# Order of the last pass, the token search, weight buffers and final stores in an attention and mixture-of-experts kernel

## The chip, the cores and the metric

The kernel runs on one core of one Trainium2 chip. The time is device microseconds of one execution; lower is better. TensorE (PE) does the matmuls, VectorE (DVE), ScalarE (ACT) and GpSimd (POOL) the rest; SyncE (SP) issues most DMAs, ACT one, and POOL the indexed ones.

## What is computed

```python
def _moe_ref(x, w_gate, w_local, w1, w2):          # x: Nystrom attention's output, 8 x 576 x 512
    ...
    for b in range(B):
        prev_e = -1
        for s in range(S):
            fresh_e = int(np.argmax(logits[b, s]))
            if s == 0 or local_gate[b, s] < 0.5:
                e = fresh_e
            else:
                e = prev_e if prev_e >= 0 else fresh_e
            prev_e = e
            ...
            h = np.maximum(x[b, s] @ w1[e], 0.0)
            out[b, s] = p[e] * (h @ w2[e])
```

The attention part has 32 landmarks per head, a softmax of three score matrices and six Newton steps for a pseudo-inverse. Each token is then sent through one of eight experts (512 to 1024 to 512). In most batches nearly all tokens have the same expert.

## The kernel before

Each batch is run with its own most frequent expert, as two passes over its tokens (`PASSES`): tokens 256 to 575 (blocks 2, 3 and the half block 4), then tokens 0 to 255 (blocks 0 and 1). Tokens with another expert are collected over all batches into slots of 128 tokens, one expert each. With these inputs one slot is enough; its **slot pass** follows the last batch, and a loop for more slots stands behind it (`tc.If(n_slots > 1)`), which is not entered.

A pass has eight steps, one per block `f` of the hidden dimension. Step `f` does `mm1` (six matmuls into a PSUM bank `ph` of which there are two; ACT writes the rectified high part `h` at L938, DVE the low part at L943 and, for the half block, L946) and, a step or two later, `after` (six matmuls into two banks `py`: `wh` with high `h`, `wl` with high `h`, `wh` with low `h`). In the slot pass it is three matmuls. All weights and activations are split into a high and a low float32r part. `split_w2` makes `wh` by a cast on ACT (L918) and `wl` by a subtraction on POOL (L920); `w_w1` folds the attention's weights into the first layer and writes `gh` (ACT) and `gl` (DVE, L906). Raw blocks of w2 have four buffers, `wh` and `wl` eight each.

The order on all engines is written by hand: `at_time(t, fn)` puts an event on a clock that has one unit per step of a pass, 16 per batch (`CH`), and `run` emits what is due before the next step's matmuls. A generator's `yield d` puts its rest `d` units later. Each engine executes its instructions in the order emitted.

For the slot, `slot_tokens` (from L1058) finds on DVE which tokens are in it: a first part up to the registers `xregs` (L1061 to L1070), a second that ends with `row` and `rhs` (L1073 to L1088), five small matmuls (L1092), the addresses `gi` (L1095 to L1108), eight gathers on POOL (L1113), and the transposition of what they brought, `xa` (L1119). `slot_weights` reads the registers on SP and loads `xwt` and w1. Before the change these events stood at

```python
    at_time((B - 1) * CH + 5.5, slot_tokens, sts[B])
    at_time((B - 1) * CH + 6, slots_end)
```

that is, in the first pass of the last batch, and the slot's weights were handled in the second pass. At the end `slot_store` scales the slot's result on ACT and DVE, half each (L1136, L1137), and POOL scatters it to its rows (L1138). Results of whole blocks are scaled on ACT (L1000) and stored by SP (L1002); the half block 4 goes over ACT (L1008, L1009) and POOL (L1011).

Of the kernel before, what the change touches and what calls it, by code (L numbers as in the profile page):

```python
# [23 lines left out]
P = 128  # L24
# [38 lines left out]
def nystrom_attn_then_sticky_moe(ctx, tc, qT, kT, v, wg, w12, out):  # L63
# [821 lines left out]

    def w_w1(st, q, f0=0, nf=4, banks=((pg, "pg"), (ph, "ph"))):

# [11 lines left out]
        if f0 == 0:  # L899
            st["g", q] = [fw.tile([P, 2, 512], F32R, name=f"g{p}", bufs=3) for p in "hl"]  # L900
        gh, gl = st["g", q]
# [11 lines left out]

    def split_w2(w2, f, by=nc.scalar.copy):

        raw = w2[f]
        wh, wl = w2[f] = [fw.tile([P, 512], F32R, name=f"w{p}", bufs=8) for p in "hl"]
        by(out=wh, in_=raw)  # L918
        yield 0.25
        nc.gpsimd.tensor_tensor(out=wl, in0=raw, in1=wh.bitcast(F32), op=ALU.subtract)  # L920

# [69 lines left out]
    def catch_up():  # L991
        run(math.inf)
        while behind:
            behind.pop(0)()

    def store(b, st, k, yp):
        t0 = b * S + k * P
        if k < 4:
            ys = fk.tile([P, DM], F32, name="ys", bufs=2)
            nc.scalar.mul(out=ys, in_=yp, mul=st["pw"][:, k:k + 1])  # L1000
            yield 0.5
            nc.sync.dma_start(out=out[t0:t0 + P, :], in_=ys)  # L1002
        else:
# [54 lines left out]
    def slot_tokens(st):  # L1058
# [26 lines left out]
        for i in range(3, 6):  # L1085
            nc.vector.tensor_copy(out=rhs[:, :, i], in_=p)
            if i < 5:
                nc.vector.tensor_tensor(out=p, in0=p, in1=rhs[:, :, i], op=ALU.subtract)  # L1088
        yield 1.25
        pi = one.tile([P, 6])  # L1090
# [20 lines left out]
        for g in range(2):  # L1111
            for c in range(4):
                nc.gpsimd.indirect_dma_start(out=xa[:, g, c, :], out_offset=None, in_=ad,  # L1113
                                             in_offset=bass.IndirectOffsetOnAxis(ap=gi[:, g, c:c + 1], axis=0),
                                             bounds_check=B * P * 2 * NJ - 1, oob_is_err=False)
        yield 6.5
        px = one.tile([P, 2, P])
# [5 lines left out]

    def slot_weights(st):
        e = expert_of(xregs[0:1, 0:1])
        b = nc.values_load(xregs[0:1, 1:2], engines=[ET.SP], min_val=0, max_val=B - 1,
                           skip_runtime_bounds_check_because="a batch")
        st["wt"] = xp.tile([P, 2, P], F32, name="xwt")
        nc.sync.dma_start(out=st["wt"], in_=wtd[bass.ds(b, 1)].rearrange("a p (g x) -> p (a g) x", g=2))
        for hf in range(2):  # L1130
            st["w1", hf] = load_w1(e, hf)
        return e
# [101 lines left out]
    for b in range(1, B):  # L1234
        attention(b)
    for b in range(1, B + 1):
        t0 = (b - 1) * CH
        for hf in range(2):
            at_time(t0 + (G0, G1)[hf] + ((b == 1) * 1, 1.5 * (b in (B - 2, B - 1)))[hf], lambda b=b, hf=hf: w_w1(sts[b], hf))
        for f in range(NC2):  # L1240
            at_time(t0 + W2 + f + (b == 1), get_w2, b, f)
            at_time(t0 + C2 + 1.75 * (b == 1) + 0.9 * f, cast_w2, b, f)
    for f in range(NC2):
# [21 lines left out]
    def slots_end():  # L1265
        sts[B]["e"] = slot_weights(sts[B])

# [3 lines left out]
    at_time((B - 2) * CH + 11.75, tables, B - 1, 1, 0.5)  # L1271
    at_time((B - 1) * CH + 5.5, slot_tokens, sts[B])
    at_time((B - 1) * CH + 6, slots_end)

    with tc.manual_schedule():
        startup(sts[0], sts[1])
        for b in range(B):
            st = sts[b]
            gen = expert(st, w2s[b], PASSES, lambda k, yp, b=b, st=st: store(b, st, k, yp), b == 0)
            for i in range(CH):  # L1280
                if i % NC2 != 3:
                    clock[0] = b * CH + i
                    run(clock[0])
                next(gen)
        st = sts[B]
        gen = expert(st, w2s[B], ((0, P, (0,)),), lambda k, yp: slot_store(st, k, yp))
        for f in range(NC2):
            if f != 3:
                clock[0] = B * CH + f
                run(clock[0])  # L1290
            next(gen)
        catch_up()
# [34 lines left out]
```

## Time and profile before

| | |
|---|---|
| median of 3 runs | 465.86 us (465.59 to 466.44) |
| the profiled execution | 466.5 us in all, of which the span of its instructions 464.7 us |
| TensorE busy | 446.7 us, 96% of the span |
| VectorE, ScalarE, GpSimd busy | 290.0, 208.8 and 194.1 us |
| granted TensorE clock, mean | 0.996 of full speed |
| DMA | 82.58 MB, 178 GB/s over the span |

All times in the rows below count from the start of the span. Busy time of TensorE is modelled from pipelined matmuls, so that a short hole does not show as idle. The first pass of the last batch runs from 400.6 to about 422, its second pass to 447, the slot pass to 457.3.

### The profile page before, as it was taken

The page shows a single profiled execution, that of the slowest core. Times are in us where ns is not written, and L with a number is a line of the kernel's source. Part 1 is how long each engine was busy: PE and PEld are TensorE (multiplying, and loading weights), DVE is VectorE, ACT ScalarE, POOL GpSimd, SP SyncE. Part 2 cuts the span into 40 slices and gives each one's busy share as a digit, 9 for nine tenths or more (in the row PEclk, how much of TensorE's full clock was granted, in tenths as well). Part 3 has the DMA queues.
Part 4 walks back from the last instruction along what each step waited for, and adds up shares of the span by engine and source line. Part 5 has one row for each costly group of instructions (what it writes and reads, how often), then busy time and mean ns, then how long its engine had stood idle before and what let it go on. Part 6 is the DMA issues. An engine that isn't in the chain of part 4 may idle for free. (4 is left out here: it accounts for less than half of the span.)

```text
span 464.7 us, 12032 instructions
## 1 busy us (share of the span) xinstructions
PE 446.7 (96%) x4688; PEld 338.4 (73%) x4688; DVE 290.0 (62%) x862; ACT 208.8 (45%) x538; POOL 194.1 (42%) x216
## 2 busy tenths in 40 slices
PE   8888999999999999999999999999999999999993
PEld 2435667777787788777887788778878788788772
DVE  7875888767476765857575775857356756335230
ACT  2526435555363724555254724554255414532450
POOL 5455471246343632256235622364016601534561
PEclk9999999999999999999999999999999999999998
DMA  8669925647345851859054941762073305616430
GB/s 305 215 205 333 336 94 175 237 135 279 142 150 202 282 201 44 288 167 329 10 211 162 310 155 50 281 210 91 2 279 120 131 0 202 217 47 214 139 138 21
DMA packets 38812, 82.58 MB, mean 178 GB/s; under 512 B 3243, under 2 KB 4523, under 8 KB 37984
## 3 DMA queue, kind: packets, MB, share of 16 engines
q1 hardware_dynamic: 37184, 76.58, 47.7%
q0 software_dynamic: 1488, 5.07, 3.1%
q8 instruction: 38, 0.62, 0.6%
q14 instruction: 22, 0.18, 0.1%
q10 hardware_dynamic: 80, 0.13, 0.1%
HBM read 66.34 MB, written 15.47 MB: 176 GB/s over the span
## 5 line engine op out<-in xcount | busy, mean ns | idle before, releaser
L973 PE MATMUL py<-wh,h 128*128 128x512 f32 x528 | 171.7, 407 | 0.0
L920 POOL TENSOR_TENSOR wl<-raw,wh 128x512 fp32r<-128x512 f32 x72 | 92.6, 1293 | 95.2 <-ACT wh L918 91.3
L938 ACT ACTIVATE h<-ph 128x256 fp32r<-128x256 f32 (+2 forms) x136 | 54.4, 401 | 162.1 <-PE ph L931 123.3
L973 PEld LDWEIGHTS py<-wh,h 128*128 128x128 f32 x528 | 89.3, 188 | 27.1 <-issue 15.2
L943 DVE SCALAR_TENSOR_TENSOR h<-ph,h 128x256 fp32r<-128x256 f32 (+1 forms) x136 | 55.5, 409 | 81.9 <-ACT h L938 76.3
L973 PE MATMUL py<-wl,h 128*128 128x512 f32 x264 | 83.2, 393 | 0.0
L931 PE MATMUL ph<-ath,gh 128*128 128x320 f32 (+1 forms) x256 | 76.9, 300 | 1.2 <-ACT gh L903 0.6
L931 PE MATMUL ph<-ath,gl 128*128 128x320 f32 (+1 forms) x256 | 75.6, 295 | 0.0
L931 PE MATMUL ph<-atl,gh 128*128 128x320 f32 (+1 forms) x256 | 75.6, 295 | 0.0
L973 PEld LDWEIGHTS py<-wl,h 128*128 128x128 f32 x264 | 49.4, 188 | 11.8 <-POOL wl L920 0.8
L931 PEld LDWEIGHTS ph<-ath,gh 128*128 128x128 f32 x256 | 48.3, 189 | 9.6 <-ACT h L938 1.1
L931 PEld LDWEIGHTS ph<-atl,gh 128*128 128x128 f32 x256 | 48.2, 188 | 4.5
L931 PEld LDWEIGHTS ph<-ath,gl 128*128 128x128 f32 x256 | 48.2, 188 | 0.2 <-DVE gl L906 0.2
L918 ACT CAST wh<-raw 128x512 fp32r<-128x512 f32 x69 | 42.5, 620 | 1.2 <-DMA raw<-w 1.2
L234 POOL TENSOR_TENSOR t<-q_t 128x288 f32<-128x288 f32 x20 | 14.6, 747 | 38.4 <-DVE before L560 27.6
L1011 POOL TENSOR_TENSOR ys<-ys,yl 64x512 f32<-64x512 f32 x8 | 10.3, 1284 | 43.1 <-ACT yl L1009 43.1
L234 POOL TENSOR_TENSOR t<-k_t 128x288 f32<-128x288 f32 x20 | 14.5, 748 | 28.8 <-DVE sq L236 18.1
L906 DVE TENSOR_TENSOR gl<-pg,gh 128x512 fp32r<-128x512 f32 (+2 forms) x19 | 12.4, 655 | 17.4 <-ACT gh L903 17.4
L1000 ACT ACTIVATE ys<-py,token 128x512 f32<-128x512 f32 x32 | 20.3, 686 | 5.8 <-PE py L973 5.8
L982 PE MATMUL pg<-wh,h 128*128 128x512 f32 x56 | 22.0, 392 | 0.0
L982 PE MATMUL pg<-wl,h 128*128 128x512 f32 x56 | 21.9, 391 | 0.0
L492 POOL TENSOR_TENSOR sa<-sa,rsa 128x1152 f32<-128x1152 f32 x7 | 14.9, 2135 | 14.2 <-PE one L445 11.7
(330 smaller groups left out, 702.8 us busy)
## 6 DMA issues: line engine op xcount, KB each, us to landing
raw<-w SPq DMA_DIRECT2D x73, 256.0 KB, 7.3
raw<-w SPq DMA_DIRECT2D x17, 1024.0 KB
v_t<-v SPq DMA_DIRECT2D x8, 1024.0 KB, 5.8
out<-ys SPq DMA_DIRECT2D x32, 256.0 KB, 3.0
q_t<-qT SPq DMA_DIRECT2D x6, 1152.0 KB, 8.3
k_t<-kT SPq DMA_DIRECT2D x6, 1152.0 KB
ad<-sa POOLq DMA_DIRECT2D x8, 576.0 KB
q_t<-qT SPq DMA_DIRECT2D x3, 576.0 KB
```

Source lines behind the costliest of these rows:

```text
L234: nc.gpsimd.tensor_add(t9[:, i], src[:, a + i, :, 0:9], src[:, a + i, :, 9:18])
L492: nc.gpsimd.tensor_tensor(out=sa, in0=sa, in1=rs.unsqueeze(2).broadcast_to([P, 2 * NJ, M]), op=ALU.mult)
L906: nc.vector.tensor_tensor(out=gl[:, g, x], in0=ps[g], in1=gh[:, g, x].bitcast(F32), op=ALU.subtract)
L918: by(out=wh, in_=raw)
L920: nc.gpsimd.tensor_tensor(out=wl, in0=raw, in1=wh.bitcast(F32), op=ALU.subtract)
L931: mm = nc.tensor.matmul(hp, w[:, g, c], x[:, g, s0:s0 + n], start=(i == 0), stop=(i == 5))
L938: nc.scalar.activation(out=h[:, 0:e], in_=hp[:, 0:e], func=AF.Relu)
L943: nc.vector.scalar_tensor_tensor(out=h[:, 384:384 + m], in0=hp[:, 0:m], scalar=0.0, in1=h[:, 0:m].bitcast(F32), op0=ALU.max, op1=ALU.subtract)
L973: nc.tensor.matmul(yps[k], h[:, part + i * P:part + i * P + P], w, start=(f == 0 and part == 0 and w is wh), stop=(f == NC2 - 1 and part = ...
L982: nc.tensor.matmul(yps[4], hs[ff][1], w, start=(ff == 0 and w is w2[ff][0]), stop=(ff == NC2 - 1 and w is w2[ff][1]))
L1000: nc.scalar.mul(out=ys, in_=yp, mul=st["pw"][:, k:k + 1])
L1011: nc.gpsimd.tensor_tensor(out=ys[0:64], in0=ys[0:64], in1=yl[0:64], op=ALU.add)
```

## The change

The slot pass moves between the two passes of the last batch. `slot_tokens` is due 7.25 units earlier (in the second pass of the batch before), `slot_weights` 6.5 units earlier, with the second half of w1 three units after the first. The slot's `w_w1` take PSUM banks of the pool `psa`; its second `gh` and `gl` and its `wh` and `wl` (seven of eight) have buffers of their own in the pool `xp`. For blocks 4 to 7 of the last batch `wl` is made on DVE in place of POOL. The last two results are blocks 0 and 1 of the last batch: block 0 is scaled on DVE and stored by SP, block 1 is scaled on ACT and stored by ACT's own queue. `catch_up` now alternates between events and deferred matmuls.

```diff
@@ -883,7 +883,7 @@
                 "a f p x -> p (a f) x"))
         return t
 
-    def w_w1(st, q, f0=0, nf=4, banks=((pg, "pg"), (ph, "ph"))):
+    def w_w1(st, q, f0=0, nf=4, banks=((pg, "pg"), (ph, "ph")), home=fw):
 
 
         w1 = st["w1", q]
@@ -897,7 +897,7 @@
                 nc.tensor.matmul(ps[g][32 * c:32 * c + 32, :], st["wt"][r, g, 32 * c:32 * c + 32],
                                  w1[r, f0:f0 + nf, a * P:a * P + P], start=True, stop=True)
         if f0 == 0:
-            st["g", q] = [fw.tile([P, 2, 512], F32R, name=f"g{p}", bufs=3) for p in "hl"]
+            st["g", q] = [home.tile([P, 2, 512], F32R, name=f"g{p}", bufs=3 if home is fw else 1) for p in "hl"]
         gh, gl = st["g", q]
         for g in range(2):
             nc.scalar.copy(out=gh[:, g, x], in_=ps[g])
@@ -911,13 +911,13 @@
         nc.sync.dma_start(out=raw, in_=w12[bass.ds(e, 1), f, :, 512:1024].rearrange("a p x -> p (a x)"))
         return raw
 
-    def split_w2(w2, f, by=nc.scalar.copy):
+    def split_w2(w2, f, by=nc.scalar.copy, rest=nc.gpsimd, home=fw):
 
         raw = w2[f]
-        wh, wl = w2[f] = [fw.tile([P, 512], F32R, name=f"w{p}", bufs=8) for p in "hl"]
+        wh, wl = w2[f] = [home.tile([P, 512], F32R, name=f"w{p}", bufs=8 if home is fw else 7) for p in "hl"]
         by(out=wh, in_=raw)
         yield 0.25
-        nc.gpsimd.tensor_tensor(out=wl, in0=raw, in1=wh.bitcast(F32), op=ALU.subtract)
+        rest.tensor_tensor(out=wl, in0=raw, in1=wh.bitcast(F32), op=ALU.subtract)
 
     def mm1(st, hs, f, s0, n, apart):
 
@@ -989,17 +989,21 @@
                 yield
 
     def catch_up():
-        run(math.inf)
-        while behind:
-            behind.pop(0)()
+        while behind or events:
+            run(math.inf)
+            if behind:
+                behind.pop(0)()
 
     def store(b, st, k, yp):
         t0 = b * S + k * P
         if k < 4:
             ys = fk.tile([P, DM], F32, name="ys", bufs=2)
-            nc.scalar.mul(out=ys, in_=yp, mul=st["pw"][:, k:k + 1])
+            if b == B - 1 and k == 0:
+                nc.vector.tensor_scalar(out=ys, in0=yp, scalar1=st["pw"][:, k:k + 1], scalar2=None, op0=ALU.mult)
+            else:
+                nc.scalar.mul(out=ys, in_=yp, mul=st["pw"][:, k:k + 1])
             yield 0.5
-            nc.sync.dma_start(out=out[t0:t0 + P, :], in_=ys)
+            (nc.scalar if b == B - 1 and k == 1 else nc.sync).dma_start(out=out[t0:t0 + P, :], in_=ys)
         else:
             p = st["pw"][0:64, k:k + 1]
             yield 2
@@ -1086,7 +1090,7 @@
             nc.vector.tensor_copy(out=rhs[:, :, i], in_=p)
             if i < 5:
                 nc.vector.tensor_tensor(out=p, in0=p, in1=rhs[:, :, i], op=ALU.subtract)
-        yield 1.25
+        yield 1.75
         pi = one.tile([P, 6])
         for k in range(NBLK):
             nc.tensor.matmul(pi, row[:, k, :], rhs[:, k, :], start=(k == 0), stop=(k == NBLK - 1))
@@ -1113,7 +1117,7 @@
                 nc.gpsimd.indirect_dma_start(out=xa[:, g, c, :], out_offset=None, in_=ad,
                                              in_offset=bass.IndirectOffsetOnAxis(ap=gi[:, g, c:c + 1], axis=0),
                                              bounds_check=B * P * 2 * NJ - 1, oob_is_err=False)
-        yield 6.5
+        yield 5.25
         px = one.tile([P, 2, P])
         for g in range(2):
             nc.tensor.transpose(out=px[:, g, :], in_=xa[:, g].rearrange("p c l -> p (c l)"), identity=ident)
@@ -1121,13 +1125,13 @@
         nc.scalar.copy(out=st["at"][0], in_=px)
         nc.vector.tensor_tensor(out=st["at"][1], in0=px, in1=st["at"][0].bitcast(F32), op=ALU.subtract)
 
-    def slot_weights(st):
+    def slot_weights(st, parts=(0, 1)):
         e = expert_of(xregs[0:1, 0:1])
         b = nc.values_load(xregs[0:1, 1:2], engines=[ET.SP], min_val=0, max_val=B - 1,
                            skip_runtime_bounds_check_because="a batch")
         st["wt"] = xp.tile([P, 2, P], F32, name="xwt")
         nc.sync.dma_start(out=st["wt"], in_=wtd[bass.ds(b, 1)].rearrange("a p (g x) -> p (a g) x", g=2))
-        for hf in range(2):
+        for hf in parts:
             st["w1", hf] = load_w1(e, hf)
         return e
 
@@ -1233,13 +1237,16 @@
     G0, G1, W2, C2 = 13.75, 16.75, 11, 14
     for b in range(1, B):
         attention(b)
-    for b in range(1, B + 1):
+    for b in range(1, B):
         t0 = (b - 1) * CH
         for hf in range(2):
             at_time(t0 + (G0, G1)[hf] + ((b == 1) * 1, 1.5 * (b in (B - 2, B - 1)))[hf], lambda b=b, hf=hf: w_w1(sts[b], hf))
         for f in range(NC2):
             at_time(t0 + W2 + f + (b == 1), get_w2, b, f)
-            at_time(t0 + C2 + 1.75 * (b == 1) + 0.9 * f, cast_w2, b, f)
+            if b == B - 1 and f > 3:
+                at_time(t0 + C2 + 0.9 * f, lambda f=f: split_w2(w2s[B - 1], f, rest=nc.vector))
+            else:
+                at_time(t0 + C2 + 1.75 * (b == 1) + 0.9 * f, cast_w2, b, f)
     for f in range(NC2):
         if f > 3:
             at_time(f - 3, get_w2, 0, f)
@@ -1263,14 +1270,24 @@
         nc.gpsimd.memset(xs["now"], 0.0)
 
     def slots_end():
-        sts[B]["e"] = slot_weights(sts[B])
+        sts[B]["e"] = slot_weights(sts[B], (0,))
+
+    def slot_w1():
+        sts[B]["w1", 1] = load_w1(sts[B]["e"], 1)
 
     xp = None
     at_time((B - 2) * CH + 0.5, slots_begin)
     at_time((B - 2) * CH + 2.5, tables, 0, B - 1, 0.75)
     at_time((B - 2) * CH + 11.75, tables, B - 1, 1, 0.5)
-    at_time((B - 1) * CH + 5.5, slot_tokens, sts[B])
-    at_time((B - 1) * CH + 6, slots_end)
+    last = (B - 1) * CH
+    at_time(last - 1.75, slot_tokens, sts[B])
+    at_time(last - 0.5, slots_end)
+    at_time(last + 2.5, slot_w1)
+    for hf in range(2):
+        at_time(last + (5.25, 8.5)[hf], lambda hf=hf: w_w1(sts[B], hf, banks=((psa, "one"), (psa, "one")), home=(fw, xp)[hf]))
+    for f in range(NC2):
+        at_time(last + 3 + 0.75 * f, get_w2, B, f)
+        at_time(last + 6.25 + 0.75 * f, lambda f=f: split_w2(w2s[B], f, home=xp))
 
     with tc.manual_schedule():
         startup(sts[0], sts[1])
@@ -1278,17 +1295,17 @@
             st = sts[b]
             gen = expert(st, w2s[b], PASSES, lambda k, yp, b=b, st=st: store(b, st, k, yp), b == 0)
             for i in range(CH):
+                if b == B - 1 and i == NC2:
+                    slot = expert(sts[B], w2s[B], ((0, P, (0,)),), lambda k, yp: slot_store(sts[B], k, yp))
+                    for f in range(NC2):
+                        if f != 3:
+                            clock[0] = last + NC2 + f
+                            run(clock[0])
+                        next(slot)
                 if i % NC2 != 3:
-                    clock[0] = b * CH + i
+                    clock[0] = b * CH + i + NC2 * (b == B - 1 and i >= NC2)
                     run(clock[0])
                 next(gen)
-        st = sts[B]
-        gen = expert(st, w2s[B], ((0, P, (0,)),), lambda k, yp: slot_store(st, k, yp))
-        for f in range(NC2):
-            if f != 3:
-                clock[0] = B * CH + f
-                run(clock[0])
-            next(gen)
         catch_up()
     n_slots = nc.values_load(nslot[0:1, 0:1], min_val=0, max_val=E * B * 5)
     with tc.If(n_slots > 1):
```

Lines from L997 on have numbers higher by 4 or more in the changed kernel: the comparison that makes `row` is L1080 before and L1084 after, the small matmuls L1092 and L1096.

The first place is DVE's list where the second pass of the batch before the last ends: `h` rows are low parts of steps, and the row ahead of the first one shown is the second `gl` subtraction. Before:

```order
L906 TENSOR_TENSOR gl_5826<-ph_5816,gh_5825 128x512
L943 SCALAR_TENSOR_TENSOR h_5845<-ph_5838,h_5845 128x256
L943 SCALAR_TENSOR_TENSOR h_5867<-ph_5860,h_5867 128x256
L943 SCALAR_TENSOR_TENSOR h_5889<-ph_5882,h_5889 128x256
L946 SCALAR_TENSOR_TENSOR h_5889<-ph_5882,h_5889 128x64
L943 SCALAR_TENSOR_TENSOR h_5913<-ph_5906,h_5913 128x256
```

After, from the first of these `h` rows on (six operations of the search, L1065 to L1074, now stand between the `gl` row and it):

```order
L943 SCALAR_TENSOR_TENSOR h_5845<-ph_5838,h_5845 128x256
L1077 TENSOR_SCALAR mask_5862<-xslot_5365,xnow_5367 128x40
L1079 TENSOR_TENSOR m3_5864<-token_126,mask_5862 128x120
L1081 TENSOR_REDUCE mine_5866<-m3_5864 128x15
L1084 TENSOR_TENSOR row_5884<-iota128_84,mine_5866 128x640
L1087 TENSOR_TENSOR rhs_5886<-tab_93,mine_5866 128x5x3
L1090 CAST rhs_5886<-mine_5866 128x5
L1092 TENSOR_TENSOR mine_5866<-mine_5866,rhs_5886 128x5
L1090 CAST rhs_5886<-mine_5866 128x5
L1092 TENSOR_TENSOR mine_5866<-mine_5866,rhs_5886 128x5
L1090 CAST rhs_5886<-mine_5866 128x5
L943 SCALAR_TENSOR_TENSOR h_5882<-ph_5875,h_5882 128x256
```

The low part of the next step (`h_5867` before, `h_5882` after) had nothing between it and the step before; now the second part of the search stands there.

The second place is TensorE's list at the same point, between `after` of a step and the next `mm1`. Before:

```order
L973 MATMUL py_5724<-wh_5500,h_5845 128x512
L973 MATMUL py_5725<-wh_5500,h_5845 128x512
L931 MATMUL ph_5906<-ath_5760,gh_5825 128x320
L931 MATMUL ph_5906<-atl_5761,gh_5825 128x320
L931 MATMUL ph_5906<-ath_5760,gl_5826 128x320
```

After:

```order
L973 MATMUL py_5725<-wl_5501,h_5845 128x512
L973 MATMUL py_5724<-wh_5500,h_5845 128x512
L973 MATMUL py_5725<-wh_5500,h_5845 128x512
L1096 LDWEIGHTS row_5884
L1096 MATMUL one_5939<-rhs_5886,row_5884 128x6
```

Four more such pairs of L1096 follow, and then the same `mm1` as before, now into `ph_5946`. The five small matmuls that read `row` and `rhs` came four steps later before; `ph_5906` and `ph_5946` are the bank that the low part `h_5867` or `h_5882` sets free.

The third place is the end of ACT's list. Before:

```order
L938 ACTIVATE h_6479<-ph_6472 128x128
L938 ACTIVATE h_6492<-ph_6485 128x128
L938 ACTIVATE h_6505<-ph_6498 128x128
L1136 ACTIVATE ys_6517<-py_6442,xpw_6143 128x256
L1293 TENSOR_LOAD nslot_129
```

After:

```order
L938 ACTIVATE h_6480<-ph_6473 128x256
L938 ACTIVATE h_6496<-ph_6489 128x256
L1004 ACTIVATE ys_6519<-py_6427,token_126 128x512
L1006 DMA out<-ys_6519 128x512
L1310 TENSOR_LOAD nslot_129
```

Where half a slot tile was scaled for POOL's scatter, a whole block is scaled and stored by ACT itself; DVE's last instruction is likewise a block of 128x512, and SP's last DMA its store.

## Rows read from the trace of the kernel before

**Rows 1.** Busy time by windows, one window: us, busy time of each engine (instructions), clock, DMA, GB/s.
```profile
410.00:420.00 10.00, 10.00 (x52) 8.68 (x51) 3.98 (x16) 1.86 (x5) 3.48 (x3) 1.00 0.00 0
```

**Rows 2.** Timeline of the end: start us, us, engine line operation out<-in, [idle before].
```profile
456.90 0.39 PE L973 MATMUL py<-wh,h 128*128 128x512 f32 x1
457.33 0.47 ACT L1136 ACTIVATE ys<-py,xpw 128x256 f32<-128x256 f32 x1 [1.84 <-PE py L973]
457.90 0.48 DVE L1137 TENSOR_SCALAR ys<-py,xpw 128x256 f32<-128x256 f32 x1 [2.09 <-ACTq L1294]
458.67 1.03 POOL L1138 DMA_INDIRECT out<-ys,tis  x1 [4.87 <-DVE ys L1137]
```

**Rows 3.** Sequencer at L1294 and L1323: ns min/median/max, first and last start us.
```profile
L1294 POOLq INC_SWDGE_SEM  x1: 531/531/531, 461.9 to 461.9; - x1
...
L1323 POOLq DRAIN  x3: 40/107/1462, 462.4 to 464.5; - x3
L1323 SPq DRAIN  x3: 7/7/13, 463.1 to 464.2; - x3
```

**Rows 4.** Tile ys from 400 us on: scaling of whole blocks, landing of stores.
```profile
L1000 ACT ACTIVATE ys<-py,token x6: 680/684/690, 405.1 to 448.1; 128x512 f32<-128x512 f32 x6
...
DMA to landing us min/median/max: 2.1/2.3/3.0
```

**Rows 5.** Timeline of DVE, the token search in its old place.
```profile
416.81 0.14 DVE L1061 TENSOR_SCALAR xnow<-xnow 128x1 f32<-128x1 f32 x1
...
418.24 0.16 DVE L1070 CAST xregs<-xv 1x2 int32<-1x2 f32 x1
...
419.65 0.81 DVE L1080 TENSOR_TENSOR row<-iota,mine 128x640 bf16<-128x640 bf16 x1
...
421.28 0.18 DVE L1086 CAST rhs<-mine 128x5 bf16<-128x5 f32 x1
```

**Rows 6.** Timeline of DVE around the new place of the search.
```profile
396.82 0.68 DVE L906 TENSOR_TENSOR gl<-ph,gh 128x512 fp32r<-128x512 f32 x1
...
399.83 0.42 DVE L943 SCALAR_TENSOR_TENSOR h<-ph,h 128x256 fp32r<-128x256 f32 x1 [0.60 <-ACT h L938]
```

**Rows 7.** Timeline of TensorE, first matmuls of two steps of the last batch.
```profile
402.86 0.30 PE L931 MATMUL ph<-ath,gh 128*128 128x320 f32 x1
...
407.42 0.38 PE L931 MATMUL ph<-ath,gh 128*128 128x320 f32 x1 [0.25 <-DVE h L946]
```

**Rows 8.** Timeline of POOL, splits of the last batch's w2.
```profile
398.57 3.81 POOL L920 TENSOR_TENSOR wl<-raw,wh 128x512 fp32r<-128x512 f32 x3 [6.32 <-ACT wh L918]
402.70 1.30 POOL L920 TENSOR_TENSOR wl<-raw,wh 128x512 fp32r<-128x512 f32 x1 [0.32 <-ACT wh L918]
```

**Rows 9.** Timeline around 391 us, POOL and DVE.
```profile
390.95 1.29 POOL L1011 TENSOR_TENSOR ys<-ys,yl 64x512 f32<-64x512 f32 x1 [19.39 <-ACT yl L1009]
...
391.06 1.21 DVE L1037 TENSOR_SCALAR xend<-xend 128x8 f32<-128x8 f32 x1
```

**Rows 10.** Two lines of DVE over the whole span: ns min/median/max.
```profile
L564 DVE TENSOR_TENSOR ecol<-ecol,low x8: 166/539/547, 29.7 to 383.0; 128x5 int32<-128x5 int32 x8
...
L943 DVE SCALAR_TENSOR_TENSOR h<-ph,h x136: 282/424/426, 38.7 to 455.5; 128x256 fp32r<-128x256 f32 x128, 128x128 fp32r<-128x128 f32 x8
```

**Rows 11.** Timeline of POOL's gathers, first and last of eight, and of DVE.
```profile
423.39 1.10 POOL L1113 DMA_INDIRECT xa<-ad,gi  x1 [7.87 <-DVE fx L1101]
...
432.65 1.00 POOL L1113 DMA_INDIRECT xa<-ad,gi  x1 [0.30 <-issue]
...
423.46 0.16 DVE L1106 TENSOR_TENSOR tis<-fx 128x1 int32<-128x1 f32 x1
```

**Rows 12.** Timeline of ACT, casts of blocks 5 and 6 of the last batch.
```profile
408.90 1.13 ACT L918 CAST wh<-raw 128x512 fp32r<-128x512 f32 x2
```

**Rows 13.** Busy time by windows, two windows after the last matmul: columns as in rows 1.
```profile
457.30:461.00 3.70, 0.00 (x0) 0.00 (x0) 0.48 (x1) 0.47 (x1) 1.03 (x1) 1.00 0.18 63
461.00:464.70 3.70, 0.00 (x0) 0.00 (x0) 0.00 (x0) 0.00 (x0) 0.00 (x0) 0.51 0.01 2
```

## The prediction

> **What bounds the kernel.** I read the windows first: in the last batch TensorE is busy the whole stretch [rows 1], as in every window up to 457. So the time is TensorE's list of work plus the tail behind its last matmul. The change adds and removes no matmul; it can only shorten the tail or open holes in TensorE's list.
>
> The tail comes from the timeline of the end [rows 2] and the sequencer's rows [rows 3]. TensorE ends at 457.29. ACT scales one half of the slot tile from 457.33, DVE the other half to 458.38, POOL issues the scatter to 459.70, and its landing lets POOL go on at 461.9. Then SP works through its list of semaphores (from 462.4, its first drain at 463.1), POOL drains from 462.4 to 463.9, and 0.8 us of barriers end the span at 464.7. The tail is 464.7 - 457.3 = 7.4 us.
>
> **The change, step by step.**
>
> *Plain stores at the end.* The last result is now two blocks of 128x512. Counted from the same point (457.33): ACT scales its block in 0.69 us [rows 4] to 458.02 and issues the store about 0.05 later. DVE scales the other block beside it: 0.48 us for 256 columns [rows 2], so at most 0.96 by twice that, and it starts one matmul (0.23) earlier, so it ends hardly later than ACT. Stores land 2.1 to 3.0 us after issue [rows 4]; two at once move 512 KB, so I take 2.4, which gives 460.5. Then SP's semaphores (462.4 to 463.1, 0.7 us, plus some 0.3 for those ahead of them) and the barriers (0.8): 462.3. POOL's long drain, 1.46 us, is done before, since POOL no longer waits for a scatter. Gain 464.7 - 462.3 = **-2.4**; with landings of 2.1 and 3.0 it is -2.7 and -1.8.
>
> *The token search moves forward.* In the old place DVE ran it from 416.81 to 421.46 [rows 5], 4.65 us with one step's h pieces inside, and POOL idle. Now it stands on DVE right behind the second gl subtraction, which ends at 397.50 [rows 6]; undisturbed it would end at about 402.0, with one h piece inside. TensorE would not feel it: the h piece behind the search (the row at 399.83) would end at 402.4, and the matmul that needs its PSUM bank comes at 402.86 [rows 7].
>
> But in the new place POOL is splitting w2: three subtractions back to back from 398.57 to 402.38, a fourth from 402.70 to 404.00 [rows 8]. The trace shows what that does. A tensor_scalar of 128x8 on DVE took 1.21 us because it started while POOL's addition of 390.95 to 392.24 ran; it ended 0.03 behind it [rows 9]. L564, two inputs in SBUF, takes 0.17 us alone and 0.54 in most batches, where it meets POOL's additions; L943, which has one input in PSUM, never takes over 0.43 [rows 10]. So an operation of DVE with two SBUF inputs, or a tensor_scalar or cast from SBUF to SBUF, waits for the end of the POOL instruction that runs when it comes, and back-to-back POOL instructions catch each one that waits on the one before.
>
> Worked through: the first six operations take 1.59 us [rows 5]; the sixth, the cast to xregs, starts at 398.9 and is held to 399.87. The h piece that stands here follows to 400.3 (it is needed by the last pair of matmuls ahead of 402.86: free). The mask comes into POOL's second split and ends at 401.15, m3 into the third, to 402.5, the sum takes 0.37 to 402.9. The comparison that makes row (0.81) comes into the fourth and ends at about 404.7. The small rest takes 421.46 - 420.46 = 1.0, to 405.7; no fifth split follows, since splits 4 to 7 leave POOL. Then the h piece, 0.42, to 406.1. TensorE wants to go on at 402.86 with the five small matmuls that read row, and then with the mm1 that needs that h piece's bank: it goes on at 406.1. Less the 0.14 of the five matmuls, which ran before at another place, a hole of 3.1 us. If the cast to xregs is not held, the phase shifts by one POOL instruction: mask 399.9, m3 401.3, row 403.1, one more hold to 404.3 by the split that row itself delayed, and the end at 405.7: 2.8. I take **+2.9**. The lower bound is 0 (no holds), the upper one 4.2 (one POOL instruction more, 1.27).
>
> *Splits 4 to 7 of the last batch on DVE.* Each at most 0.68 (the gl subtraction of the same size [rows 6]). The first of them, and ahead of it the nine operations from pf to xpw (0.16 each or a little more with their waits [rows 11], some 1.4 us), stand before the h piece for which TensorE already waited at 407.42 [rows 7]: **+0.2**. It runs beside the gathers. In the trace a two-input operation ran its usual 0.16 during a gather of 1.10 [rows 11], so I take no hold; the bound is one gather there, +0.6. The Trainium skill, SBUF — State Buffer, Who interferes with whom, says a tensor_tensor with two SBUF inputs contends only with GpSimd instructions that read SBUF, and infers that writing descriptors is not among them; by it the sum stays, and no run here shows it for 512 columns.
>
> *Gathers.* Eight at 1.30 us, 423.39 to 433.65 [rows 11], 10.3 us. With the hole they start at about 409 and end near 419.5; they are read behind mm1 of the pass's last block, at 421.0 + 1.0 (the slot's first w_w1, moved ahead) + 3.1 = 425. Nothing, unless landing takes over 5 us. POOL's eight slot splits (1.27 each) then run from 419.6 to 430, with TensorE's first use at about 434: nothing. Without the hole all of this shifts together.
>
> *Loads.* The slot's xwt and first half of w1 now stand on SP ahead of the loads of w2 blocks 5 to 7; blocks 5 and 6 are cast at 408.90 [rows 12], over 6 us behind the splits that free their buffers (401.1 and 402.4 [rows 8]); that hides the 1.1 MB now ahead of them. Nothing; were it too short, the cast would hold the h pieces behind it on ACT. In the slot pass ACT has the last three casts and the scaling of the pass's block 4 (two operations) in a row ahead of h pieces; its steps are the shortest, so I bound this by +0.6 and take 0.
>
> **Sum:** 2.9 + 0.2 - 2.4 = +0.7 (rounded to +0.6, as the slot's w_w1 no longer wait for a bank, some 0.1). The profiled execution: span 464.7, in all 466.5, so 467.1; the median of the runs lies 0.64 below it at 465.86: **466.5**, +0.1%. This case's own range is 465.6 to 467.6. A measurement of this kernel tells about 0.2%, or 0.93 us, from no change.
>
> **Rivals.**
>
> *No hole (faster, 463.7).* The search's operations are too short or of the wrong kind to be held, or POOL's splits come later than the search. For it: TENSOR_REDUCE and PSUM inputs are not held; the first four operations just end before 398.57. Against it: the mask, m3 and row are of the kinds that waited. Then 0 + 0.3 - 2.4 = -2.1. Chance 0.30.
>
> *The last two stores land late (slower, 467.3).* Both are issued within 0.1 us, and the longest landing in the last stretch is 3.0 [rows 4]. Then the tail gives 1.8, and with a hole of 3.1: 3.1 + 0.2 - 1.8 = +1.5. It decides from a landing of some 2.7 us on, since then the sum passes +0.93. For it: two equal stores share the same engines. Against it: the median is 2.3. Chance 0.25, a hole over 3.2 us from another hold, with the same sum, included.
>
> *The clock falls in the hole (slower, 469 or more).* TensorE's granted clock stayed 1.00 from 457.3 to 461.0, 3.7 us without a matmul, and was 0.51 behind that [rows 13]: from 2.4 to 1.2 GHz. The hole is cut by the five small matmuls and shorter than that. If it were longer, one step of the pass (2.7 us) at half clock would add 2.7. Chance 0.05. The Trainium skill, TensorE: Matmul & The Clock Gate, What's actually happening, has the gate fall behind an idle stretch; the tail agrees (0.51), and by that rule alone this case would be the slower one.
>
> **Numbers.** Forecast 0.40, no hole 0.30, late stores 0.25, clock 0.05. The range takes most of the second and third: 463.3 to 467.8. The forecast's own case lies within 0.2% nearly always; a little of it is slower. Faster by over 0.2%: 0.30; within: 0.38; slower: 0.32.
>
> **What would show it.** After the last matmul some 5.0 us to the end instead of 7.4, with POOL out of it. On DVE, mask, m3 and row stretched to the ends of POOL's splits, and row over 1.5 us. On TensorE, a hole of about 3 us ahead of the five small matmuls, clock at 1.00. A search that ends by 402.5 makes the second step wrong, and the time faster; a hole at the transposes of xa or in the slot pass would be one that I did not count.

## The result and the profile after

The changed kernel takes 469.20 us (median of 6 runs, 467.66 to 471.42) against 465.88 us before: ratio 1.0069, 95% interval 1.0050 to 1.0087. It is slower, by 3.3 us. The prediction said 466.5 (463.3 to 467.8), with no change as the likeliest.

The profiled execution of the changed kernel took 467.66 us, the shortest of its six; span 465.9 us. TensorE is busy for 446.9 us, as before (446.7); its last matmul ends at 459.89 instead of 457.29. The span ends 6.0 us behind it instead of 7.4. So the tail is shorter by 1.4, and TensorE's list is longer by more than that.

Where it got longer: the timeline of DVE and of POOL in the new place of the search, in the changed kernel (start us, us, engine line operation). They answer to [rows 6] and [rows 8].

```profile
396.25 0.68 DVE L906 TENSOR_TENSOR gl<-ph,gh 128x512 fp32r<-128x512 f32 x1
...
397.64 1.42 DVE L1071 TENSOR_TENSOR which<-eb,og 128x128 f32<-128x128 f32 x1
...
399.42 0.82 DVE L1074 CAST xregs<-xv 1x2 int32<-1x2 f32 x1
400.16 0.40 DVE L943 SCALAR_TENSOR_TENSOR h<-ph,h 128x256 fp32r<-128x256 f32 x1
400.50 1.00 DVE L1077 TENSOR_SCALAR mask<-xslot,xnow 128x40 f32<-128x40 f32 x1
...
402.26 0.82 DVE L1084 TENSOR_TENSOR row<-iota,mine 128x640 bf16<-128x640 bf16 x1
403.00 1.24 DVE L1087 TENSOR_TENSOR rhs<-tab,mine 128x15 bf16<-128x15 f32 x1
404.15 0.16 DVE L1090 CAST rhs<-mine 128x5 bf16<-128x5 f32 x1
...
405.04 0.75 DVE L943 SCALAR_TENSOR_TENSOR h<-ph,h 128x256 fp32r<-128x256 f32 x2
```

And POOL:

```profile
397.62 3.84 POOL L920 TENSOR_TENSOR wl<-raw,wh 128x512 fp32r<-128x512 f32 x3 [6.56 <-ACT wh L918]
402.82 1.38 POOL L920 TENSOR_TENSOR wl<-raw,wh 128x512 fp32r<-128x512 f32 x1 [1.37 <-ACT wh L918]
```

POOL's three splits end near 398.9, 400.2 and 401.46, the fourth at 404.20. L1071 ends at 399.06, the cast at 400.24, the mask at 401.50, `rhs` at 404.24: each 0.02 to 0.15 behind the end of a split. The search ends at 405.1; with the 4.65 us of its old place [rows 5], counted from its start at 396.85 here, it would have ended at 401.5. The `h` piece behind it starts at 405.04.

TensorE in the same stretch (the bracket is idle time and what ended it):

```profile
395.80 0.39 PE L931 MATMUL ph<-ath,gh 128*128 128x256 f32 x1 [0.25 <-DVE h L943]
...
400.62 0.41 PE L931 MATMUL ph<-ath,gh 128*128 128x320 f32 x1 [0.36 <-DVE h L943]
...
405.19 0.27 PE L1096 MATMUL one<-rhs,row 128*128 128x6 bf16 x5 [2.04 <-DVE rhs L1090]
```

The first of these matmuls stands in the kernel before, too, ahead of everything that was moved:

```profile
396.29 0.39 PE L931 MATMUL ph<-ath,gh 128*128 128x256 f32 x1 [0.17 <-DVE h L943]
```

From there to the last matmul it is 457.29 - 396.29 = 61.0 us before and 459.89 - 395.80 = 64.1 after: **+3.1 us** on TensorE. By the last matmul ahead of the hole (402.53, and 402.40 before) 0.6 of it is there, with the wait of 0.36 above in it. The other 2.5 lie between it and the next `mm1` (405.51, and 402.86 before): the hole of 2.0, the small matmuls and the restart behind them.

The end, timeline of all engines:

```profile
459.76 0.75 DVE L1002 TENSOR_SCALAR ys<-py,token 128x512 f32<-128x512 f32 x1 [3.10 <-PE py L973]
459.93 0.69 ACT L1004 ACTIVATE ys<-py,token 128x512 f32<-128x512 f32 x1 [3.72 <-PE py L973]
460.54 0.34 SPq L1006 DMA_DIRECT2D out<-ys  x1
460.65 0.36 ACTq L1006 DMA_DIRECT2D out<-ys  x1
```

SP sees the first store at 463.7 (3.2 us after issue) and the second at 464.0 (3.35), works through its list to 465.0, and the barriers end at 465.9. POOL is out of it, as forecast.

This one execution is +1.2 us over that of before. The terms give 3.1 - 1.4 = +1.7; the other 0.5 lies ahead of the search, to which this execution came that much sooner (395.80 against 396.29). The median is +3.3. Part of what is missing shows in the clock column of the six runs: mean granted clocks of 0.996, 0.999 and 0.999 go with 467.66, 468.73 and 467.78 us, and 0.994, 0.993 and 0.992 with 471.42, 469.88 and 469.66.

### The profile page after: what moved, and what is told of

It reads as the page before. It is cut to its first block, busy times and chain, and to the rows that moved or that the text cites. A ratio compares the mean times of both kernels' runs of the same rounds, so it can differ in the third digit from the quotient of the medians.

```text
span 465.9 us, 12017 instructions
## 1 busy us (share of the span) xinstructions
PE 446.9 (96%) x4688; PEld 338.3 (73%) x4688; DVE 296.7 (64%) x867; ACT 208.1 (45%) x537; POOL 189.6 (41%) x212
## 4 chain that ended last, share of the span: by engine, by line
PE 81%; DVE 8%; DMA 3%; issue 3%; POOL 1%; ACT 1%; SPq 1%; DVEq 0%; POOLq 0%; ACTq 0%
PE py L973 37%; PE ph L931 21%; PE pg L982 6%; PE one L429 3%; PE one L368 2%; DMA raw<-w 2%; PE one L469 2%; PE one L385 2%; PE ph L897 2%; PE one L333 1%; DMA k_t<-kT 1%; PE one L517 1%; PE pg L897 1%; POOL wl L920 1%; DVE sk L230 1%
## 5 line engine op out<-in xcount | busy, mean ns | idle before, releaser
L920 POOL TENSOR_TENSOR wl<-raw,wh 128x512 fp32r<-128x512 f32 x68 | 87.6, 1295 | 90.0 <-ACT wh L918 89.6
L906 DVE TENSOR_TENSOR gl<-pg,gh 128x512 fp32r<-128x512 f32 (+2 forms) x17 | 11.0, 650 | 14.2 <-ACT gh L903 12.8
```

The source lines that it names most:

```text
L920: rest.tensor_tensor(out=wl, in0=raw, in1=wh.bitcast(F32), op=ALU.subtract)
```

## The experiments

Two questions were open. What makes the hole: operations held by POOL's splits, or simply the length of the search on DVE? And what sets the median 1.5 us over the profiled execution: **theory A**, TensorE's granted clock falls behind the hole in some executions; **theory B**, some load or store lands late in them.

**The changed kernel again.** No edit. e1_again ran beside the next three kernels, e11_after beside the last three.

> The changed kernel once more, to see what sets its runs apart (467.7 to 471.4 us in six). Theory A, the hole ahead of the five small matmuls lets TensorE's granted clock fall in some runs: long runs have a lower mean clock (0.992 to 0.994 against 0.996 to 0.999), and a profile of one shows a stretch at 1.2 GHz behind 405 us. Theory B, a load or a store that lands late in some runs: long and short runs have the same mean clock, and the extra stands as an idle stretch of TensorE elsewhere or as a longer tail.

> The changed kernel as it is, for comparison with e10_fill7 on the same chip: 469.2 to 469.6, about two runs in three with a mean clock of 0.989 to 0.995, these some 1.8 us longer than the others.

Measured: 469.52 (468.62 to 470.95) and 469.60 (468.02 to 470.24). Of all 18 runs of this kernel, 12 have a mean clock of 0.994 or less; their median is 469.9. The other six (0.996 or more): 468.3. The mean clock tells only roughly whether it fell: a profile of e4_tail below has a fall at a mean of 0.995. The profile of e11_after is one of the twelve. Its windows (us, busy time of PE, PEld, DVE, ACT, POOL, then clock, DMA share, GB/s):

```profile
399.00:403.00 4.00, 4.00 (x22) 3.19 (x20) 3.90 (x6) 2.16 (x5) 3.68 (x4) 1.00 0.40 100
403.00:405.70 2.70, 0.05 (x1) 0.10 (x1) 2.56 (x8) 0.00 (x0) 0.99 (x1) 1.00 0.90 310
405.70:406.80 1.10, 1.03 (x10) 0.94 (x10) 0.74 (x3) 0.00 (x0) 0.00 (x0) 1.00 1.02 356
406.80:410.20 3.40, 3.40 (x11) 2.82 (x10) 2.16 (x12) 1.61 (x4) 0.77 (x1) 0.50 0.48 183
410.20:414.20 4.00, 3.81 (x32) 2.57 (x32) 1.96 (x6) 2.92 (x8) 3.09 (x4) 1.00 0.56 159
```

TensorE stands idle from 403.05 to 405.72, starts again at 1.00, and 1.1 us later is granted 0.50 (1.2 GHz) for 3.4 us: 11 matmuls in the fourth window. From the small matmuls to the last one it is 54.43 us in the profiles of the change and e1_again (no fall) and 55.88 in e11_after: the fall costs 1.45 us, and step by step it comes to 1.4 and 1.5 in the profiles of e4_tail and e7_one below. The Trainium skill, TensorE: Matmul & The Clock Gate, What's actually happening, has the gate fall behind an idle stretch: these traces agree.

The whole stretch is longer in those two, 56.51 in e7_one and 56.87 in e4_tail. The other 0.6 and 1.0 us arise later, at full clock, at the slot's first `w_w1` (L897), whose weight loads come there in two pieces instead of one. TensorE's weight loads, the change and then e7_one:

```profile
418.51 0.18 PEld L897 LDWEIGHTS one<-raw,xwt 64*32 64x32 f32 x16 [0.19 <-issue]
```

```profile
420.48 0.14 PEld L897 LDWEIGHTS one<-raw,xwt 64*32 64x32 f32 x4 [0.19 <-issue]
421.02 0.23 PEld L897 LDWEIGHTS one<-raw,xwt 64*32 64x32 f32 x12 [0.40 <-issue]
```

What interrupts them no trace shows. So the clock is not all that sets the runs apart.

**The second part of the search later.** In `slot_tokens`:

```diff
-    def slot_tokens(st):
+    def slot_tokens(st, late=2.0):
...
-        yield 0.5
+        yield late
         mask = xp.tile([P, NCOL], F32, name="mask")
...
-        yield 1.75
+        yield 1.0
         pi = one.tile([P, 6])
...
-        yield 5.25
+        yield 4.5
         px = one.tile([P, 2, P])
```

> The second part of the token search (mask to rhs) starts 1.5 steps later, behind POOL's fourth split; the rest of the change is kept. If the holds by POOL's splits make the hole (my theory): row takes 0.8 us and the rest its usual times, the hole of 2.0 us ahead of the five small matmuls is under 0.3, the time is 465.0 to 465.6, and, by theory A, the runs lie within 0.6 us of each other. If the search's own length on DVE makes the hole: a hole of over 1 us stands one or two steps later, and the time stays at 467 or more. By theory B the hole goes, but the runs still spread by 2 us or more and the median is near 466.7.

Measured: 466.76 (465.92 to 467.94, 12 runs), not the 465.0 to 465.6 expected. The move was one step too short: mask, `m3` and `row` still met POOL's splits (0.69, 1.33 and 1.63 us), and 0.90 us of the hole was left. DVE's timeline of e2_late2, and POOL's fourth split:

```profile
402.59 1.63 DVE L1084 TENSOR_TENSOR row<-iota,mine 128x640 bf16<-128x640 bf16 x1
```

```profile
402.24 1.30 POOL L920 TENSOR_TENSOR wl<-raw,wh 128x512 fp32r<-128x512 f32 x1 [0.60 <-ACT wh L918]
```

Against the change's undisturbed 468.3 the time fell by 1.5 us, and the hole by 1.1 to 1.8. With 11 of 12 mean clocks at 0.996 or more, the falls had all but gone. But the spread of 2.0 us and the median are what theory B had forecast: something holds some runs up at full clock too, and this experiment does not tell what.

**Later still.** The mask 3.0 units behind the first part, and the small matmuls and the addresses `gi` ahead of the second `w_w1`'s `gl`. Against e2_late2 (two further waits, ahead of the gathers and of the transposes, change by a quarter unit and are not shown):

```diff
-    def slot_tokens(st, late=2.0):
+    def slot_tokens(st, late=3.0):
...
-        yield 1.0
+        yield 0.45
         pi = one.tile([P, 6])
...
-        yield 0.5
+        yield 0.04
         pf = xp.tile([P, 6], F32, name="pf")
```

> The search's second part stands another step later than in e2_late2, so that only the fourth split of POOL meets its first operation; the five small matmuls stand just ahead of the second w_w1 and the addresses right behind them. Holds theory: mask alone is held (to about 403.6), row takes 0.8 us, the wait ahead of the five small matmuls is under 0.4 us, no fall of the clock, mean clock 0.995 or more in nearly all runs; PE's end 1.0 to 1.4 us sooner than in e2_late2 (458.2), time 464.8 to 465.6. Rival, the search is simply too long for DVE beside the h pieces: a hole of 0.8 us or more stays, at whichever place, and the time stays at 466.5.

Measured: 465.39 (464.83 to 465.85, 8 runs), ratio to before 0.9982, interval 0.9972 to 0.9992, all mean clocks 0.995 or more. The time is as expected; that `m3` and not the mask would meet the fourth split, and a wait over 0.4, were not. DVE's timeline in e5_late3, and POOL's behind it:

```profile
402.81 0.23 DVE L1077 TENSOR_SCALAR mask<-xslot,xnow 128x40 f32<-128x40 f32 x1
403.08 1.26 DVE L1079 TENSOR_TENSOR m<-token,mask 128x120 f32<-128x120 f32 x1
...
405.13 0.81 DVE L1084 TENSOR_TENSOR row<-iota,mine 128x640 bf16<-128x640 bf16 x1
405.86 0.17 DVE L1087 TENSOR_TENSOR rhs<-tab,mine 128x15 bf16<-128x15 f32 x1
```

```profile
402.89 1.31 POOL L920 TENSOR_TENSOR wl<-raw,wh 128x512 fp32r<-128x512 f32 x1 [0.17 <-ACT wh L918]
409.01 1.10 POOL L1117 DMA_INDIRECT xa<-ad,gi  x1 [4.81 <-DVE fx L1105]
```

The mask slips in between two splits (0.23 against 1.00); `m3`, which met no split in the change and took 0.28 there, meets the fourth here and takes 1.26; `row` and `rhs` find POOL quiet and take 0.81 and 0.17 (1.63 and 1.24 where they met a split). The same operations on the same tiles are long where they meet a split and short where they meet none, and in all profiles here each long one ends behind the end of a split. TensorE is left with one wait of 0.64 us. From the last matmul of this batch's first `w_w1` (L897, near 395) to the end of its list it needs 62.44 us, 63.91 in e2_late2 and 62.42 in the kernel before. Counted from the span's start that end (457.9) is only 0.3 sooner than in e2_late2, since this execution came to the search 1.1 us later. The tail is 6.2, some 1.2 shorter than before's, and the median only 0.7 lower; where the rest went is open.

**The search alone.** The kernel before, with one edit:

```diff
-    at_time((B - 1) * CH + 5.5, slot_tokens, sts[B])
+    at_time((B - 1) * CH - 1.75, slot_tokens, sts[B])
```

> The kernel before with the token search alone moved to its new place; slot pass, loads, splits and stores stay. Holds: the same stretched mask, row and rhs, a hole of 2.0 to 2.9 us, tail 7.4: 468.2 to 468.8 in a run with an undisturbed clock. Theory A: median above that, some runs near 470 at a lower mean clock. Theory B: all runs within 0.6 us of 468.5, since the loads stand where they stood. If the move of the slot pass made the hole: no hole, 465.9.

Measured: 472.84 (472.21 to 475.73, 5 runs), mean clocks 0.984 to 0.994. The stretched search is there without the slot pass being moved, so the search makes the hole (3.58 us here). But the time is some 3 us over what any theory had; the profile is that of the longest run, and it shows a second hole. TensorE, ACT and DVE in e3_early:

```profile
405.43 0.28 PE L1092 MATMUL one<-rhs,row 128*128 128x6 bf16 x5 [3.58 <-DVE rhs L1086]
...
419.17 0.50 PE L982 MATMUL pg<-wh,h 128*128 128x512 f32 x1 [3.06 <-DVE gl L906]
```

```profile
417.81 0.59 ACT L903 CAST gh<-pg 128x512 fp32r<-128x512 f32 x1 [4.94 <-remote]
...
418.42 0.69 DVE L906 TENSOR_TENSOR gl<-pg,gh 128x512 fp32r<-128x512 f32 x1 [4.97 <-ACT gh L903]
```

The second hole ends with `gl` of the second `w_w1`, which waited for ACT's `gh`. ACT began that only at 417.81, over 4 us after the last L897 matmul that the trace has for its input (ended 413.36); in the kernel before it began 0.1 us after. The eight gathers (407.2 to 417.4) do stand on POOL ahead of the splits of later blocks of w2:

```profile
416.41 1.00 POOL L1113 DMA_INDIRECT xa<-ad,gi  x1 [0.30 <-issue]
417.42 1.28 POOL L920 TENSOR_TENSOR wl<-raw,wh 128x512 fp32r<-128x512 f32 x1
```

But TensorE first reads such a `wl` at 428.36, ten us behind that split's end, so it did not wait for them here. What released ACT at 417.81 is open, and whether the change's fourth edit, splits 4 to 7 on DVE, keeps this hole away is not shown. The clock fell here for 6.8 us, from 404.2, already during the first hole.

**The hole filled.** Eight (e6_fill) or seven (e10_fill7) matmuls that nothing reads, ahead of the small ones:

```diff
         yield 1.75
+        fill, g0 = one.tile([P, 512]), sts[B - 1]["g", 0][0]
+        for i in range(8):
+            nc.tensor.matmul(fill, g0[:, 0, 0:P], g0[:, 0, :], start=True, stop=True)
         pi = one.tile([P, 6])
```

> The changed kernel, with eight matmuls of 512 columns that nothing reads put ahead of the five small ones, where TensorE stood idle for 2.0 to 2.7 us; they take 8 x 0.227 = 1.8 us. The search stays held as it was. If the idle stretch lets the clock fall and that costs the median its 1.5 to 2 us: mean clock 0.995 or more in all runs, no stretch at 1.2 GHz near 405, median 467.5 to 468.2, runs within 1 us. If the spread has another cause: median 469 or more, mean clocks of 0.989 to 0.994 as before. If the hole is shorter than the fill, the surplus is added: at most 0.5.

> As e6_fill with seven matmuls in the hole instead of eight (1.6 us), beside the changed kernel itself on the same chip. The fall of the clock as the cause of most of the spread: mean clocks of 0.995 or more throughout and a median 1.0 to 1.8 us below that of e11_after. If the fall costs nothing that the median shows: the medians agree within 0.4 us though the mean clocks differ.

Measured: e6_fill 468.97 (467.96 to 470.39), e10_fill7 467.88 (467.76 to 469.44, beside e11_after's 469.60 on the same chip). Mean clocks are 0.995 to 0.999 in all twelve runs. The windows of e10_fill7, in the columns of e11_after's above:

```profile
402.00:404.80 2.80, 1.69 (x9) 1.17 (x8) 2.63 (x9) 0.00 (x0) 1.07 (x1) 1.00 0.90 311
404.80:406.00 1.20, 1.15 (x11) 1.05 (x11) 0.72 (x3) 0.00 (x0) 0.00 (x0) 1.00 1.02 357
406.00:409.40 3.40, 3.40 (x30) 2.17 (x28) 2.47 (x13) 2.54 (x5) 1.07 (x1) 1.00 0.52 194
```

`row` and `rhs` come as late as ever; only TensorE's idle time is filled, and the clock stays at 1.00. So the idle stretch lets the clock fall. What that is worth in the median is less sharp: 1.7 us in e10_fill7, as expected, but only 0.2 to 0.6 in e6_fill, which missed its 467.5 to 468.2. Three of its six runs were above 469.3 at mean clocks of 0.997 or more. So there is a second cause beside the clock, and it is open; no trace here is of such a run.

**The tail.** In e4_tail the last six matmuls go block by block:

```diff
-                    for part, w in ((0, wh), (0, wl), (384, wh)):
...
+                    trio = ((0, wh), (0, wl), (384, wh))
+                    ends = store_last and f == NC2 - 1 and blocks == (0, 1)
+                    for i, k, part, w in ([(i, k, *t) for i, k in enumerate(full) for t in trio] if ends else
+                                          [(i, k, *t) for t in trio for i, k in enumerate(full)]):
```

> The changed kernel, with the last six matmuls block by block, so that block 0 is complete 0.68 us sooner and its store is issued that much sooner. If the two stores of 256 KB delay each other (landing 3.2 us for both, 2.3 alone): block 0's store lands some 0.6 sooner, block 1's 2.6 to 2.9 us after issue, and the tail is 5.4 to 5.7 instead of 6.0. If a store at the end takes 3.2 us by itself: block 1's landing stays at 3.2 to 3.4 and the tail at 6.0. The hole stays as it is.

In e7_one one of the two last stores is left out:

```diff
-            (nc.scalar if b == B - 1 and k == 1 else nc.sync).dma_start(out=out[t0:t0 + P, :], in_=ys)
+            if b < B - 1 or k:
+                (nc.scalar if b == B - 1 and k == 1 else nc.sync).dma_start(out=out[t0:t0 + P, :], in_=ys)
```

> The changed kernel without the store of block 0 of the last batch, whose 128 rows of the output are not written; everything else stays. If two stores at once make the landing of 3.1 to 3.8 us: the remaining store lands 2.1 to 2.6 us after issue and the tail behind the last matmul is 4.9 to 5.3 us. If a store issued by ACT at this place takes that long by itself: 3.0 us or more and a tail near 5.9.

Measured: e4_tail 469.76 (467.43 to 470.45), landings 3.1 us for each of the two though they were issued 0.56 us apart, tail 5.8. e7_one, one execution, 469.98: the store that is left lands 2.9 us after issue, tail 5.7. Neither landing is what was expected of two stores that delay each other (2.6 to 2.9 for the last in e4_tail, 2.1 to 2.6 for the one in e7_one), and e7_one is nearer to a store that takes long by itself. Two at once may be part of it (3.2 to 3.8 us in the profiles with both stores issued side by side), but one alone is already 0.5 over the 2.4 that I took. The windows behind the issue, in the columns of e11_after's, first the change (two stores), then e7_one (one):

```profile
460.60:461.30 0.70, 0.00 (x0) 0.00 (x0) 0.00 (x0) 0.01 (x1) 0.00 (x0) 1.00 0.00 0
461.30:462.80 1.50, 0.00 (x0) 0.00 (x0) 0.00 (x0) 0.00 (x0) 0.00 (x0) 0.92 0.92 339
462.80:463.80 1.00, 0.00 (x0) 0.00 (x0) 0.00 (x0) 0.00 (x0) 0.00 (x0) 0.50 0.09 33
```

```profile
463.20:464.00 0.80, 0.00 (x0) 0.00 (x0) 0.00 (x0) 0.00 (x0) 0.00 (x0) 1.00 0.00 0
464.00:465.00 1.00, 0.00 (x0) 0.00 (x0) 0.00 (x0) 0.00 (x0) 0.00 (x0) 0.89 0.71 258
465.00:466.20 1.20, 0.00 (x0) 0.00 (x0) 0.00 (x0) 0.00 (x0) 0.00 (x0) 0.50 0.03 10
```

Nothing moves for 0.7 to 0.8 us, then the bulk goes at 258 to 339 GB/s, and then a last full microsecond carries 10 to 33 GB/s before the landing. Why that end is slow stays open. It need not be so: in e9_best below a whole block stored near the end lands in 2.0 us.

**Toward the best version.** e8_pi moves the small matmuls behind the second `w_w1` (0.45 becomes 0.5). e9_best adds the block order of e4_tail and scales both last blocks in halves:

```diff
+            if b == B - 1 and k < 2:
+                p, l, r = st["pw"][:, k:k + 1], slice(0, 256), slice(256, 512)
+                nc.scalar.mul(out=ys[:, l], in_=yp[:, l], mul=p)
+                nc.vector.tensor_scalar(out=ys[:, r], in0=yp[:, r], scalar1=p, scalar2=None, op0=ALU.mult)
+                for x, q in (((l, nc.scalar), (r, nc.sync)) if k else ((slice(0, 512), nc.sync),)):
+                    q.dma_start(out=out[t0:t0 + P, x], in_=ys[:, x])
+                return
```

> As e5_late3, with the five small matmuls behind the second w_w1 instead of ahead of it, so that they come 1.1 us later to row and rhs. If the 0.64 us that TensorE waited there is the last of the search's cost: it goes, and the time falls by 0.5 to 0.7 from 465.4 to 464.7 to 464.9. If the second w_w1 or the gathers then end last: the wait shows ahead of the transposes of xa or of the next mm1, and the time stays at 465.4.

> As e8_pi, with the last six matmuls block by block, both last blocks scaled in halves by ACT and DVE (0.47 us instead of 0.75), block 0 stored whole by SP and block 1 in two halves by ACT and SP. If the tail is the scaling, the landing of the last store (2.9 us alone) and the end of the program in a row: tail 5.4 to 5.6 instead of 6.0 to 6.2, time 464.1 to 464.5. If three stores share the engines so that the last lands 3.3 us or more after issue: no gain over e8_pi.

Measured: e8_pi 465.25 (464.60 to 469.56, 12 runs), ratio 0.9995, interval 0.9977 to 1.0012: no gain over e5_late3 that can be told. Its longest run, 469.56, has a mean clock of 0.992, so a fall may come without the big hole too. The wait went on to the next `mm1` (TensorE's timeline of e8_pi):

```profile
408.26 0.38 PE L931 MATMUL ph<-ath,gh 128*128 128x320 f32 x1 [0.56 <-DVE pf L1099]
```

e9_best: 464.79 (464.08 to 466.39, 9 runs), ratio 0.9980, interval 0.9969 to 0.9991, the lowest median here, though over the 464.1 to 464.5 expected, and its interval and that of e5_late3 overlap. In its profile TensorE ends at 456.86, the halves take 0.47, the whole store of block 0 lands in 2.0 us, the last half store 2.5 us after issue, and the tail is 5.4 us, as expected. Tile `ys` in e9_best from 456 us on:

```profile
DMA to landing us min/median/max: 2.0/2.3/2.5
```

## Why the prediction failed

- **The search is held by POOL's splits: right.** The kinds that I named were held to the ends of the splits. e11_after even runs the sequence that I had worked through, from a start within 0.06 us of before's (cast to 399.92, mask 401.18, `m3` 402.55, `row` 404.67, `mm1` at 406.04):

```profile
398.91 1.01 DVE L1074 CAST xregs<-xv 1x2 int32<-1x2 f32 x1
...
400.17 1.01 DVE L1077 TENSOR_SCALAR mask<-xslot,xnow 128x40 f32<-128x40 f32 x1
401.22 1.33 DVE L1079 TENSOR_TENSOR m<-token,mask 128x120 f32<-128x120 f32 x1
...
402.99 1.68 DVE L1084 TENSOR_TENSOR row<-iota,mine 128x640 bf16<-128x640 bf16 x1
```

  In the change's own profile the phase is another: `which` and `rhs` are caught, and `row` is not (0.82, where my sign was over 1.5). The end hardly differs: the hole at the small matmuls was 2.0 to 2.7 us. That 2.9 + 0.2 came out at +3.1 in that profile is partly luck, for the 0.2 was put at a step where 0.05 was found. The no-hole rival (463.7) was wrong.
- **The tail's gain of 2.4: the first step that failed.** The term was mis-sized at "I take 2.4" for the landing: it was 3.2 and 3.35 us in the profile, up to 3.8 in others, above the row's maximum of 3.0 [rows 4], and the tail gave 1.4 there, 1.0 to 1.4 in the undisturbed executions. Scaling (to 0.73 us behind the last matmul), SP's list (1.0) and the barriers (0.85) were as forecast. The rival of late stores was right, and the sum with it is 3.1 - 1.4 = +1.7.
- **The clock: the second step that failed.** I gave its fall 0.05, since the clock had held at 1.00 for 3.7 us without a matmul at the end [rows 13] and the hole was to be shorter. By the mean clocks it fell in 12 of 18 runs; in the traces it fell behind holes of 2.7 us, after TensorE had begun again. One stretch of 3.7 us showed that the clock can stay up that long; I read it as a bound below which it must. At 1.4 to 1.5 us in two runs of three it carries the median from about 468.3 to 469.2 and more. That the rival's own number, 469 or more, was met is luck: it had 2.7 for the fall.
- **What stays open.** Without the falls the runs lie at 468.3, 2.4 over before. The terms, 3.1 less the tail's 1.0 to 1.4, give 1.7 to 2.1, or 467.6 to 468.0, at the upper end of the range. The other 0.3 to 0.7 are not traced. Executions of all these kernels come to the search with up to 1.7 us between them (the last L897 matmul near 395 starts between 393.95 and 395.63; before 394.87, the change's profile 394.29), and the longer runs of e2_late2 and e6_fill show that something adds time at full clock.
- **Splits 4 to 7 on DVE** cost nothing that shows. The first ran beside a gather (408.73 to 409.83) in its usual time, timeline of DVE in the changed kernel:

```profile
408.94 0.68 DVE L920 TENSOR_TENSOR wl<-raw,wh 128x512 fp32r<-128x512 f32 x1
```

  The Trainium skill, SBUF — State Buffer, Who interferes with whom, infers that descriptor writing does not contend with such an operation; this row agrees, for 512 columns. What the edit keeps away, if anything, is not shown.
- **Gathers, loads, bank waits, slot pass:** nothing, as forecast, in the change's profile: TensorE shows no hole over 0.1 us from 411 to 459. In e7_one and e4_tail the slot's first `w_w1` took 0.6 and 1.0 us longer.

## What to carry to other kernels

Before work is moved into an engine's idle time, look at what the other engines do at that moment: the search cost TensorE 0.64 us where `row` and `rhs` met no split, and about 3 us beside the splits. Add to a stall on TensorE what its clock may take, even where one trace held the clock through a gap as long: look at the mean clock of every run, since the profiled one may be of the lucky third. Moving the consumer alone only moves the wait (e8_pi); moving the search's second part by two and a half steps made a slower change into a slightly faster kernel.

## What was not expected of the hardware

A held operation does not always end with POOL's: the mask and the cast end 0.02 to 0.04 us behind the split, `m3` 0.14, `row` 0.68 (e2_late2: 404.22, the split at 403.55), so most of a large one is still to be done then. The clock fell after the idle stretch was over: in e11_after at 406.8 us, 1.1 us behind the first matmul after a hole of 2.7 us, and in e4_tail 0.1 us behind it (405.8). It stayed at 0.50 for 3.4 us in e11_after while TensorE was full. In e3_early it fell within a hole of 3.6 us, at 404.2, for 6.8 us. And two stores of 256 KB at the very end took 3.1 to 3.8 us to land, one alone 2.9, of which the bulk was 1.5 and 1.0; yet in e9_best a whole one landed in 2.0.
